# Routed attention and a gated long convolution: keys stored negated, one mask instruction, and a new hand-out of work in the last batch

## The chip, the cores and the metric

One core of one Trainium2 chip runs the whole program. Its five engines run side by side, each from a queue of its own: TensorE (PE, the matmuls), VectorE (DVE), ScalarE (ACT), GpSimd (POOL) and SyncE (SP, which here only starts transfers). The metric is the device time of one execution in microseconds (us); a profile of one execution gives in addition the span from the first to the last instruction and a record of each of them.

## The reference

Four batches, eight heads, 768 positions of 64 numbers. Queries and keys are each assigned to the nearest of 16 centroids of their head; a query sees the keys of its own cluster alone. The attention's output, heads side by side as 512 columns, goes through a projection to three parts, of which the middle one is convolved over the whole sequence with a long filter (a circular convolution by Fourier transform), and the three are multiplied and projected out.

```python
q_assign = np.argmax(np.einsum('bhsd,hcd->bhsc', q_n, c_n), axis=-1)
k_assign = np.argmax(np.einsum('bhsd,hcd->bhsc', k_n, c_n), axis=-1)
mask = q_assign[:, :, :, None] == k_assign[:, :, None, :]
scores = scale * np.matmul(q, k.transpose(0, 1, 3, 2))
scores = np.where(mask, scores, -1000000000.0)
scores = scores - np.max(scores, axis=-1, keepdims=True)
attn = np.exp(scores)
attn = attn / (np.sum(attn, axis=-1, keepdims=True) + 1e-09)
return np.matmul(attn, v).astype(np.float32)
...
proj = x @ w_proj
x1, x2, x3 = (proj[..., :D], proj[..., D:2 * D], proj[..., 2 * D:])
X2 = np.fft.rfft(x2, n=S, axis=1)
H = np.fft.rfft(filter_fft, n=S, axis=0)[None, :, :]
x2_conv = np.fft.irfft(X2 * H, n=S, axis=1)
y = x1 * x2_conv * x3
return (y @ w_out).astype(np.float32)
```

## The kernel before

**A planner writes the order.** The program is a list of 1943 operations, each with its engine or a choice of engines, a cost in us, a due time, and what it reads and writes. `place` (line 123) simulates the engines and gives each operation its engine and its place: an engine takes, among what could start first, what is due earliest. The result is the order of every engine's queue. Two dictionaries steer it: `NUDGE` (line 42) shifts the due time of each operation, by its number in the list, and `ONLY` (line 43) fixes the engine of 134 operations that could run on several. An operation with `lock=True` takes part in a rule between DVE and POOL: a POOL operation with a lock is made to wait for the last DVE operation with a lock that stands before it in the order, so that the two don't use the memory of the core together.

**Routing** (`routing`, line 574; `first_masks` for the first group). The heads are taken in eight groups of four heads, each as two pairs. Queries and keys are loaded, transposed on PE (L594, L607), copied out of PSUM as f32 (`copy`, L282 on ACT, L284 on DVE) and cast to bf16 into the score operands `T.augs` (again `copy`; ACT, DVE or POOL). There are 64 such casts, half of them for queries (`j` = 0), half for keys (`j` = 1). The similarity to the centroids is a matmul (L627); the largest of 16 gives a one-hot row for each position. A matmul with a triangular matrix (L647) breaks ties: in its result the winner is -1 and the rest 0 or more. From this the mask rows `T.ohT` are written, in two chunks of 384 columns: rows 64 to 127 (keys) as one at the winner and zero else, rows 0 to 63 (queries) as -BIG plus BIG at the winner, with BIG = 262144. They differ, so two instructions write each chunk (L653 on ACT or L655 on DVE), 28 in the seven groups behind the first. Small transfers put the 16 rows of each head under the 64 rows of its cast operand (L497).

**Scores and values** (`attention`, line 663). The mask costs no pass of its own: the score matmul contracts over 64 + 16 rows, so a score of another cluster is 262144 lower and its exponential is zero. For each of the 96 blocks of 128 keys, PE makes three banks of scores (L84), ACT takes their exponential with scale 1/8 (L694, L697), PE multiplies with the values in f32 (L708), and DVE adds the exponentials up for the denominators (L725 for the first two blocks of a pair of heads, on DVE or POOL; L729 for the others).

**The second stage** (`hyena`, line 817), once for each batch: U projects the middle part (L843) into sums and differences (L857, L862); `spectrum4` transforms it with matmuls into six banks, three row blocks `i` by real and imaginary part `cs`. Each bank is multiplied by two rows of the filter's spectrum straight out of PSUM (L873, DVE alone, 12 a batch), and L877 combines the products into `T.y`. For each of four column blocks `dt` and two halves `ch`, G makes the two gates: the third part is copied to SBUF (L914), the first is multiplied into it straight out of PSUM (L917, DVE alone). The inverse transform `I` and its folds (L942 to L954) give the convolution, L959 multiplies it by the gates (in the last batch by halves, on DVE alone), and W projects out (L990), followed by a copy and the store. The first three batches do this beside the attention of the next ones; behind the last attention only the last batch is left, with a rest of the batch before.

The program uses PSUM as eight banks; a bank is free for the next matmul when its last reader is through, so a late reader on DVE or ACT holds PE.

Of the kernel before, what the change touches and what calls it, by code (L numbers as in the profile page):

```python
# [27 lines left out]
BIG = 262144.0  # L28
# [236 lines left out]
def build(T):  # L265
# [7 lines left out]

    def ring(n, pr):
        return (2 * n + pr) % 3

    def A(i):
        return T0 + TAU1 * min(i, NE) + TAU2 * max(i - NE, 0)

    def copy(e, out, in_):  # L280
        if e == "ACT":
            T.nc.scalar.copy(out, in_)  # L282
        else:
            (T.nc.vector if e == "DVE" else T.nc.gpsimd).tensor_copy(out, in_)  # L284

    columns = lambda *a: product(T, *a)

    def ap(h):
        return bank(h.ids[0])

    def bank(i):
        return T.bank[i][:]

    def T_(name, i):
        return lambda: getattr(T, name)[i]

    def two(h):
# [8 lines left out]
    def alu(e):  # L306
        return T.nc.vector if e == "DVE" else T.nc.gpsimd
# [194 lines left out]
    def first_masks(pr):  # L502
# [35 lines left out]
        if pr == 0:  # L538
            for j in (1, 0):
                h2 = Bank("head")  # L540

                def rows(e, j=j, h2=h2):
                    o = ap(h2).bitcast(BF16)
                    for t in range(NT):
                        for hp in range(2):
                            T.nc.tensor.transpose(o[64 - 64 * hp:80 - 64 * hp, ts(t, 128)], oh()[:, 4 * t + 2 * j + hp], T.identb)
                op(("PE", .35), rows, due + 1.0 + .1 * (1 - j), r=[("oh", 0), "identb"], w=[h2], alloc=h2, kind="sim")
                for hp in range(2):
                    def put(e, j=j, hp=hp, h2=h2):
                        rs = slice(64 - 64 * hp, 80 - 64 * hp)  # L550
                        o, x = T.augs[0][hp][j][rs], ap(h2).bitcast(BF16)[rs, :S]
                        if j:
                            copy(e, o, x)
                        elif e == "ACT":
                            T.nc.scalar.activation(o, x, Act.Copy, scale=BIG, bias=-BIG)
                        else:
                            V().tensor_scalar(o, x, BIG, -BIG, op0=Alu.mult, op1=Alu.add)
                    got = op({"ACT": .8, "DVE": .55}, put, due + 1.2 + .3 * hp, r=[h2, ("zero", 0, j)],
                             w=[("augm", 0, hp, j)], free=[h2])
            return [got]  # L560
# [13 lines left out]
    def routing(n):  # L574
# [5 lines left out]
        for u in range(8):  # L580
# [30 lines left out]
            if ch == 1:  # L611
                for hp in range(2):
                    op({"ACT": .82, "DVE": .65, "POOL": .95}, lambda e, a=ring(n, pr), hp=hp, j=j, z=z: copy(
                        e, T.augs[a][hp][j][64 * hp:64 * hp + 64],
                        T.qkT[z][64 * hp:64 * hp + 64].rearrange("p a b -> p (a b)")), due + 8 if n else due + 6,
                       r=qk(z, 0) + qk(z, 1) + [("zero", ring(n, pr), j)],
                       w=[("aug", ring(n, pr), hp, j)], lock=True)
# [27 lines left out]
        for ch in range(2):  # L645
            h = Bank(cls)
            op(("PE", .165), lambda e, ch=ch, h=h: columns(ap(h)[:, :384], T.tri[:], T.ohB[:, ts(ch, 384)], True, True), due - 2 + .1 * ch,  # L647
               r=["ohB", "tri"], w=[h], alloc=h, kind="proj")
            for j in (1, 0):
                def hits(e, ch=ch, j=j, h=h):  # L650
                    o, x = T.ohT[64 * j:64 * j + 64, ts(ch, 384)], ap(h)[64 * j:64 * j + 64, :384]
                    if e == "ACT":
# [631 lines left out]
```

## Time and profile before

| | |
|---|---|
| median of 3 runs | 370.66 us (370.66 to 370.85) |
| the profiled execution | 370.64 us |
| its span, first to last instruction | 368.9 us |
| granted TensorE clock | 1.000 throughout |
| read from and written to HBM | 31.59 and 7.40 MB |
| costliest on PE | L708, values: 143.0 us of 768 matmuls |
| on ACT | L697 and L694, exponentials: 108.7 and 57.4 us |
| on DVE | L729, sums: 112.8 us of 64 additions |
| on POOL | L284, casts: 25.9 us of 29 |

Busy times of an engine count the time in which at least one of its instructions runs. In a wait, the line after the arrow is the one whose end released the line before it; then come the total, the number and the longest. In a time line, a figure in brackets is the idle time of the engine just before the instruction, with what released it.

### The profile page before, as it was taken

To read this page: it belongs to the slowest core of one execution; us is meant where nothing else is said; L and a number is where in the kernel's file an instruction comes from. 1 tells how busy PE (TensorE), PEld (TensorE's weight loads), DVE (VectorE), ACT (ScalarE), POOL (GpSimd) and SP (SyncE) were. 2 spreads that over 40 slices of the span, in tenths; PEclk is the share of its full clock that TensorE was granted. 3 is DMA by queue.
4 is the path that set the end of the run, shared out by engine and by line. 5 is a ranking of instruction groups with operands and counts; after the bars stand their busy time and mean duration, and the time that the engine had idled before them with its cause. 6 is when DMAs were issued, how large, how long until landed. Compare 5 with 4: busy or idle time off the path is not lost.

```text
span 368.9 us, 8653 instructions
## 1 busy us (share of the span) xinstructions
PE 357.5 (97%) x3314; PEld 208.9 (57%) x3316; DVE 342.5 (93%) x478; ACT 263.6 (71%) x495; POOL 120.9 (33%) x162
## 2 busy tenths in 40 slices
PE   7899999999999999999999999999999999999985
PEld 4455544555856565565555555566555655566672
DVE  7999999896999899999999999998998999999994
ACT  7998978877986859769869765899584785433242
POOL 7730730422032752331530044352221334016610
PEclk9999999999999999999999999999999999999999
DMA  7986597484247768748556964667477750110124
GB/s 175 202 189 126 128 211 195 93 189 110 62 80 156 115 156 169 152 103 129 107 64 183 238 170 81 146 152 98 81 116 167 150 77 1 48 45 2 59 115 171
DMA packets 90405, 46.20 MB, mean 125 GB/s; under 512 B 78248, under 2 KB 84092, under 8 KB 90364
## 3 DMA queue, kind: packets, MB, share of 16 engines
q1 hardware_dynamic: 85500, 36.15, 40.5%
q0 software_dynamic: 2752, 8.98, 17.1%
q10 hardware_dynamic: 2112, 0.52, 0.6%
q8 instruction: 26, 0.43, 0.5%
q14 instruction: 15, 0.12, 0.1%
HBM read 31.59 MB, written 7.40 MB: 106 GB/s over the span
## 4 chain that ended last, share of the span: by engine, by line
PE 78%; DVE 11%; ACT 5%; issue 3%; DMA 1%; POOL 1%; SPq 0%; DVEq 0%; ACTq 0%; POOLq 0%
PE bank L84 33%; PE pair L708 28%; PE bank L843 5%; PE bank L594 5%; DVE acc L729 3%; PE bank L627 2%; ACT p L697 1%; PE bank L82 1%; DMA qkraw<-in_k_dram 1%; DVE qkP L284 1%; PE bank L475 1%; PE bank L742 1%; ACT p L694 1%; PE bank L607 1%; DVE ohT L655 1%
## 5 line engine op out<-in xcount | busy, mean ns | idle before, releaser
L708 PE MATMUL pair<-p,vraw 128*64 128x385 f32 x768 | 143.0, 489 | 0.1
L697 ACT ACTIVATE p<-bank 128x512 f32<-128x512 f32 x192 | 108.7, 606 | 23.5 <-PE bank L84 16.0
L729 DVE TENSOR_TENSOR acc<-p,acc 128x1536 f32<-128x1536 f32 x64 | 112.8, 1762 | 3.2 <-ACT p L694 0.5
L84 PE MATMUL bank<-aug,aug 80*64 80x512 bf16 (+3 forms) x736 | 81.9, 327 | 2.1 <-ACT p L697 0.9
L708 PEld LDWEIGHTS pair<-p,vraw 128*64 128x64 f32 x768 | 56.6, 136 | 43.8 <-issue 36.7
L84 PEld LDWEIGHTS <-aug 80*64 80x64 bf16 (+1 forms) x736 | 45.6, 109 | 41.0 <-issue 26.3
L694 ACT ACTIVATE p<-bank 128x512 f32<-128x512 f32 x96 | 57.4, 606 | 5.4 <-PE bank L84 3.6
L284 POOL CAST aug<-qkP 64x768 bf16<-64x768 f32 x29 | 25.9, 900 | 83.3 <-DVE acc L729 55.9
L762 POOL DMA_DIRECT2D acc<-acc x30 | 24.4, 824 | 69.8 <-DMA acc<-acc 37.4
L84 PE MATMUL bank<-xT,wpj 128*64 128x384 bf16 x504 | 47.2, 326 | 0.0
L84 PEld LDWEIGHTS <-wpj 128*64 128x64 bf16 x504 | 30.2, 110 | 14.1 <-issue 2.6
L282 ACT COPY qkP<-bank 128x512 f32<-128x512 f32 (+1 forms) x46 | 23.1, 559 | 15.9 <-PE bank L594 9.7
L84 PEld LDWEIGHTS <-y 128*64 128x64 bf16 x472 | 24.0, 110 | 13.2 <-issue 3.6
L725 POOL TENSOR_TENSOR acc<-p,p 128x512 f32<-128x512 f32 x15 | 19.3, 1297 | 32.3 <-DVE acc L729 10.4
L873 DVE TENSOR_TENSOR tm<-bank,hm 128x512 f32<-128x512 f32 x44 | 28.1, 681 | 1.9 <-POOL uv L862 0.8
L84 PE MATMUL bank<-wout,y 128*64 128x512 bf16 (+1 forms) x200 | 24.0, 371 | 1.1 <-DVE y L959 1.1
L282 ACT CAST aug<-qkP 64x768 bf16<-64x768 f32 x28 | 23.2, 830 | 1.0 <-DVE qkP L284 0.4
L843 PE MATMUL bank<-wpj,xT 128*64 128x512 bf16 x192 | 22.7, 379 | 0.4 <-ACT p L697 0.4
L725 DVE TENSOR_TENSOR acc<-p,p 128x512 f32<-128x512 f32 x33 | 21.6, 690 | 0.4 <-DMA dd<-acc 0.4
L877 POOL TENSOR_TENSOR y<-tm 128x512 bf16<-128x512 f32 x14 | 17.8, 1277 | 12.8 <-DVE tm L873 10.6
L732 ACT COPY osb<-pair 128x770 f32<-128x770 f32 x16 | 12.9, 806 | 10.8 <-PE pair L708 10.7
L594 PEld LDWEIGHTS bank<-ident,qkraw 128*128 128x128 f32 x144 | 15.6, 141 | 6.3 <-ACT p L694 2.4
(178 smaller groups left out, 435.7 us busy)
## 6 DMA issues: line engine op xcount, KB each, us to landing
vraw<-in_v_dram SPq DMA_DIRECT2D x16, 384.0 KB, 5.2
qkraw<-in_q_dram SPq DMA_DIRECT2D x30, 192.0 KB, 3.9
rb<-dr SPq DMA_DIRECT2D x30, 192.0 KB, 3.7
qkraw<-in_k_dram SPq DMA_DIRECT2D x28, 192.0 KB, 3.6
out_dram<-ob SPq DMA_DIRECT2D x9, 512.0 KB, 5.0
acc<-acc POOLq DMA_DIRECT2D x10, 384.0 KB, 4.8
acc<-acc POOLq DMA_DIRECT2D x10, 192.0 KB, 4.2
y<-in_moe_filter_fft_dram SPq DMA_DIRECT2D x4, 384.0 KB, 4.3
```

Of the source, the lines that this page charges most:

```text
L84: T.nc.tensor.matmul(out[64 * i:64 * i + 64], lhsT[:, 64 * i:64 * i + 64], rhs, start=start, stop=stop)
L282: T.nc.scalar.copy(out, in_)
L284: (T.nc.vector if e == "DVE" else T.nc.gpsimd).tensor_copy(out, in_)
L594: T.nc.tensor.transpose(bank(h.ids[i // 4])[:, ts(i % 4, 128)], raw(ss[i // NT], i % NT), T.ident[:, ::-1] if 3 <= i < NT else T.ident)
L694: T.nc.scalar.activation(o, ap(h).rearrange("p (a b) -> p a b", a=2), Act.Exp, scale=0.125)
L697: T.nc.scalar.activation(flat(s)[:, lo:lo + 512], ap(h), Act.Exp, scale=0.125)
L708: T.nc.tensor.matmul(o[64 * hp:64 * hp + 64, ch, :385], T.vraw[vs][:, hp, sk * D:(sk + 1) * D], T.p[slots[sk]][:, hp, 384 * ch:384 * ch + ...
L725: alu(e).tensor_tensor(o, x, y, op=Alu.add)
L729: T.nc.vector.tensor_tensor(T.acc[os], T.p[slots[sk]][:, :, :S], T.acc[os], op=Alu.add)
L762: op(("POOL", .8), lambda e, rows=rows: T.nc.gpsimd.dma_start(flat_()[:rows], flat_()[rows:2 * rows], accum_op=Alu.add), te, r=[], w=AK, b ...
L843: T.nc.tensor.matmul(ap(h)[64 * i:64 * i + 64], T.xT[xs][:, kt, c:c + 64], T.wpj[:, kt, DM:2 * DM], start=kt == 0, stop=kt == ND - 1)
L873: op(("DVE", .68), lambda e, i=i, cs=cs, r=r, h=h: T.nc.vector.tensor_tensor(T.tm[r][:, cs], ap(h), hmrow(i, (0, 2, 2, 3)[2 * r + cs]), op ...
```

## The change

- Keys are cast with a factor -1 (`minus` in place of `copy`), and the exponential takes the scale -1/8 in place of 1/8. The signs of the mask follow: query rows are BIG at a miss and 0 at a hit. With this sign both halves of a chunk are a relu of scale times the matmul's result plus bias, with a scale and a bias for each row, so one instruction on ACT writes all 128 rows; 28 mask instructions become 14. The two columns `T.hs` and `T.hb` are written at the start by POOL.
- In the last batch, the imaginary banks of the first two row blocks are copied to SBUF first (by ACT or DVE), into `T.acc[0]`, and their four products may run on POOL or DVE. The first-part gates of the first two column blocks are copied likewise into `T.x3`, and their four products may run on either. So may the eight last products (L959).
- The costs that the planner assumes for the casts and for L725 on DVE are changed a little, and all of `NUDGE` and `ONLY` is new (1936 operations, 136 fixed engines). The operations that stay are the same, in another order and partly on other engines.

```diff
-NUDGE = {0:-244.575,1:-2716.133,...}
-ONLY = {13:"POOL",14:"POOL",15:"POOL",...}
+NUDGE = {0:-600.355,1:-451.825,...}
+ONLY = {15:"POOL",16:"POOL",18:"POOL",...}
...
+    def minus(e, out, in_):
+        if e == "ACT":
+            T.nc.scalar.activation(out, in_, Act.Copy, scale=-1.0)
+        else:
+            alu(e).tensor_scalar(out, in_, -1.0, None, op0=Alu.mult)
...
-                    op({"ACT": .82, "DVE": .65, "POOL": .95}, lambda e, a=ring(n, pr), hp=hp, j=j, z=z: copy(
+                    op({"ACT": .83, "DVE": .56, "POOL": .9}, lambda e, a=ring(n, pr), hp=hp, j=j, z=z: (minus if j else copy)(
...
-            for j in (1, 0):
-                def hits(e, ch=ch, j=j, h=h):
-                    o, x = T.ohT[64 * j:64 * j + 64, ts(ch, 384)], ap(h)[64 * j:64 * j + 64, :384]
-                    if e == "ACT":
-                        T.nc.scalar.activation(o, x, Act.Relu if j else Act.Copy, scale=-1.0 if j else -BIG, bias=0.0 if j else -BIG)
-                    else:
-                        V().tensor_scalar(o, x, -1.0 if j else -BIG, 0.0 if j else -BIG, op0=Alu.mult, op1=Alu.max if j else Alu.add)
-                op({"ACT": .47, "DVE": .55}, hits, due - 1.6 + .1 * ch, r=[h], w=[("ohT", j, ch)], free=[h])
+            op({"ACT": .57}, lambda e, ch=ch, h=h: T.nc.scalar.activation(
+                T.ohT[:, ts(ch, 384)], ap(h)[:, :384], Act.Relu, scale=T.hs, bias=T.hb), due - 1.6 + .1 * ch,
+               r=[h, "hit"], w=[("ohT", 0, ch), ("ohT", 1, ch)], free=[h])
...
-                        T.nc.scalar.activation(flat(s)[:, lo:lo + 512], ap(h), Act.Exp, scale=0.125)
+                        T.nc.scalar.activation(flat(s)[:, lo:lo + 512], ap(h), Act.Exp, scale=-0.125)
...
-                    op({"DVE": .63, "POOL": 1.5}, part, due - 1 + .2 * u, r=[("p", slots[i], u) for i in range(2)], w=[("acc", os, u)], lock=True)
+                    op({"DVE": .68, "POOL": 1.5}, part, due - 1 + .2 * u, r=[("p", slots[i], u) for i in range(2)], w=[("acc", os, u)], lock=True)
...
+                away = last and cs and i < 2
+                if away:
+                    spec, sk = (lambda i=i: T.acc[0][:].rearrange("p a b -> p (a b)")[:, ts(i, 512)]), [("acc", 0, i)]
+                    op(EV512, lambda e, spec=spec, h=h: copy(e, spec(), ap(h)), due + 1, r=[h], w=sk, free=[h])
+                else:
+                    spec, sk = (lambda h=h: ap(h)), [h]
                 for r in range(2):
...
+                    op({"DVE": .68, "POOL": 1.4} if away else ("DVE", .68), lambda e, i=i, cs=cs, r=r, spec=spec: alu(e).tensor_tensor(
+                        T.tm[r][:, cs], spec(), hmrow(i, (0, 2, 2, 3)[2 * r + cs]), op=Alu.mult), due + 1 + .1 * r,
+                       r=sk + [("hm", i, ((0, 2), (2, 3 if i == 0 else 0))[r][cs])], w=[("tm", r, cs), ("tm", r)],
+                       free=[] if away else [h], lock=away)
...
+                    elif last and dt < 2:
+                        op(EV384, lambda e, ch=ch, dt=dt, h=h: copy(e, T.x3[dt][:, ch], ap(h)[:, :384]), due + .8,
+                           r=[h], w=[("x3", dt, ch)], free=[h])
+                        op({"DVE": .55, "POOL": 1.1}, lambda e, ch=ch, dt=dt, x3=x3: alu(e).tensor_tensor(
+                            x3()[:, ch], T.x3[dt][:, ch], x3()[:, ch], op=Alu.mult), due + 1.4,
+                           r=[("x3", dt, ch)], w=xkeys[ch], lock=True)
...
-                op(("DVE", .55) if last else {"DVE": .95, "POOL": 2.1}, lambda e, dt=dt, ch=ch, cols=cols, x3=x3, yy=yy: alu(e).tensor_tensor(
+                op({"DVE": .55, "POOL": 1.1} if last else {"DVE": .95, "POOL": 2.1}, lambda e, dt=dt, ch=ch, cols=cols, x3=x3, yy=yy: alu(e).tensor_tensor(
...
+        def hit(e):
+            for j in range(2):
+                G().memset(T.hs[64 * j:64 * j + 64], -1.0 if j else BIG)
+                G().memset(T.hb[64 * j:64 * j + 64], 0.0 if j else BIG)
+        op(("POOL", .4), hit, 16, w=["hit"])
```

## The prediction

> **What bounds the kernel now.** I read the page first, its busy rows and its chain of waits.
>
> ```profile
> PE 357.5 (97%) x3314; PEld 208.9 (57%) x3316; DVE 342.5 (93%) x478; ACT 263.6 (71%) x495; POOL 120.9 (33%) x162
> ...
> PE 78%; DVE 11%; ACT 5%; issue 3%; DMA 1%; POOL 1%; SPq 0%; DVEq 0%; ACTq 0%; POOLq 0%
> ```
>
> TensorE (PE) works 357.5 of 368.9 us and holds 78% of the chain. The change touches no matmul: the scores, the value products, the gates and the transforms keep their number and their shapes. So whatever it takes off VectorE (DVE) or ScalarE (ACT) shortens the kernel only where PE now stands still. Where that is I read from the busy time of each engine in stretches of 12 us; the columns are PE, PEld, DVE, ACT, POOL, clock, DMA share, GB/s.
>
> ```profile
> 0.00:12.00 12.00, 9.20 (x46) 4.72 (x47) 9.30 (x28) 8.70 (x17) 8.99 (x41) 1.00 0.82 185
> 12.00:24.00 12.00, 11.25 (x114) 6.63 (x113) 11.29 (x22) 11.38 (x23) 7.33 (x20) 1.00 0.88 188
> 24.00:36.00 12.00, 11.25 (x98) 6.69 (x96) 11.21 (x12) 10.85 (x23) 0.82 (x1) 1.00 0.74 156
> ...
> 60.00:72.00 12.00, 11.57 (x93) 6.27 (x92) 10.92 (x15) 10.49 (x20) 3.42 (x3) 1.00 0.56 130
> ...
> 108.00:120.00 12.00, 11.53 (x97) 6.91 (x94) 11.79 (x13) 8.33 (x17) 3.23 (x4) 1.00 0.81 160
> ...
> 240.00:252.00 12.00, 11.25 (x132) 8.21 (x128) 11.34 (x16) 10.94 (x21) 5.02 (x5) 1.00 0.72 158
> ...
> 348.00:360.00 12.00, 10.93 (x178) 8.33 (x176) 11.85 (x24) 5.04 (x11) 3.40 (x3) 1.00 0.22 90
> 360.00:369.00 9.00, 4.63 (x44) 2.08 (x40) 3.46 (x8) 2.52 (x5) 0.00 (x0) 1.00 0.47 175
> ```
>
> PE's holes, twelve (or nine) minus the first busy number: 2.80 and 0.75 at the start, 0.75 in 24 to 36, 0.43 in 60 to 72, 0.47 in 108 to 120, 0.75 in 240 to 252, 1.07 in 348 to 360, 4.37 at the end. The stretches left out add 0.15. That is 11.54 us, the whole budget. The 4.37 is mostly the last eviction and the last store behind the last matmul, which the change leaves; most of the 2.80 is the wait for the first loads. In play are about 4.2 us between 12 and 360, and some of the 2.80.
>
> Two of the holes have a name in the waits of PE:
>
> ```profile
> PE bank L84 <- DVE y L959: 1.1, 1, 1.1
> ...
> PE bank L84 <- DVE ohT L655: 0.7, 1, 0.7
> ```
>
> **The merged mask instruction.** Each of the seven later routings writes its masks with four instructions, two for each half of the rows: L653 and L655, 28 in all.
>
> ```profile
> L655 DVE TENSOR_SCALAR ohT<-bank x7: 542/560/561, 32.6 to 280.7; 64x384 bf16<-64x384 f32 x7
> ...
> L653 ACT ACTIVATE ohT<-bank x21: 471/485/500, 31.4 to 269.5; 64x384 bf16<-64x384 f32 x21
> ```
>
> They take 21 x 0.485 + 7 x 0.560 = 14.1 us. Afterwards 14 instructions on ACT alone write all 128 rows of 384 elements, with scale and bias from columns. No row shows that form. Below it lies the plain 128x384 ACT copy of L282 (0.48); above it the 128x512 activation with a scale column of L451 (0.688). I take 0.58, near the middle: 14 x 0.58 = 8.1 us (6.7 to 9.6). Six us of engine time go, 3.9 of them DVE's. Almost all of it is hidden, since PE is full beside it. It shows once: at 32.58 two L655 run on DVE, held until two accumulations of L729 (29.04, 3.62 us) are through; ACT's second mask waits 0.8 for the bank and PE's next score stands 0.66. With masks on ACT alone nothing of this queue is left, so I count -0.7 (0 to -0.75, the whole hole of 24 to 36). What ACT does instead, 0.58 in place of 0.485, delays the exponentials queued behind it by 0.1, which PE has banks to ride out. The four column writes of the new constants run on GpSimd (POOL), like L1044's 0.09 each: some 0.3 us, needed only at 31 us, where POOL has stood 3.7 us idle before 20.3. Nothing; uncovered, it is +0.3.
>
> **Negated keys.** 32 of the 64 casts into the score operands become a multiplication by -1. On ACT the form is in the trace: L1069 writes 64x768 bf16 from f32 as an activation in 0.83, the cast of L282 takes 0.831. On DVE the cast takes 0.548; the nearest multiplication from SBUF, L381 with 128x384, takes 0.41, which doubled is 0.82: 0.55 to 0.82, and I take the cast, the row of the same shape. On POOL the cast takes 0.82, a two-input 128x512 operation 1.277, or 1.9 for 768: 0.82 to 1.9, and I take 0.82, since there is still one input. The sign in the exponential costs no instruction; L697's 0.602 stays. So 0, with +0.8 on the dear side, should one slow POOL cast in the start lie before the first scores (the rows at 14.67 and 15.76).
>
> **The last batch.** Two spectral results and four gate results are first copied to SBUF, by ACT at 0.587 and 0.480: 2 x 0.59 + 4 x 0.48 = 3.1 us. ACT is busy 8.03 of the 23 us from 337 to 360, so they are hidden; on DVE they would be 3.6. Then up to four spectral products (0.68), four gate products (0.55) and all eight last products (0.55) may go to POOL. The dictionary of fixed engines names one spectral product and one gate product for POOL; of the others the diff doesn't tell. Those two take 0.62 + 0.47 = 1.1 us off DVE, by the distance between starts in a train (4 products of L873 in 2.47; 2 of L917 in 1.01). DVE is busy 22.71 of 23.00 there, so this arrives at its end, and its end holds PE:
>
> ```profile
> 357.87 0.28 PE L84 MATMUL bank<-wout,y 128*64 128x256 bf16 x2
> 359.22 5.41 PE L84 MATMUL bank<-wout,y 128*64 128x256 bf16 x54 [1.07 <-DVE y L959]
> ```
>
> PE waits 1.07 for a product of L959, then works through the output projection without a pause. More than 1.07 can't be won here: without the wait PE itself is the end. I take -0.7, two thirds, because POOL's price comes back in part (next). Bounds: -1.07 and +2.4 (rival 2).
>
> A row speaks against these moves. A DVE operation with two inputs in SBUF is stretched when POOL works beside it: L729 goes from 1.754 to 2.592, L725 from 0.684 to 1.022. One with an input in PSUM isn't: L873 stays at 0.68, though most of its 48 run beside POOL. The copies turn PSUM inputs into SBUF ones, and the kernel makes such POOL operations wait for the DVE ones (the lock). The Trainium skill says the same in general (GPSIMD Engine Reference, section 4.1, Engine selection): elementwise work belongs on VectorE, about twice as slow on GpSimd for two inputs; this trace has 1.277 against 0.685, a ratio of 1.9. By that rule the tail would gain nothing and the sum would be -0.7 instead of -1.4.
>
> **The new order.** All due times change and some 170 engine choices are set, freed or set otherwise. PE's work stays at 357.5 minus or plus a few changes of array shape (a value product behind a transpose takes 1.45, else 1.30). What an order can still win are the holes without a name: 0.43 + 0.47 + 0.75 in the middle and perhaps 1 us at the start; what it can lose is as much. I take 0, -1.6 to +1.6.
>
> **Sum.** Profiled execution 370.64, its span 368.9, 1.7 around it; the median is 370.66, so the two agree. -0.7 (masks) + 0 (keys) - 0.7 (tail) + 0 (order) = -1.4: 369.2; I write 369.3.
>
> **Rivals.**
> 1. *The order pays the gain back.* The two named holes go, and others of their size open elsewhere, since PE has only 0.15 us of idle in the 22 stretches left out above and any late operand shows at once. For it: the waits of PE are ten rows of different places, nine of them a single wait each. Against: nothing in the diff adds work to PE's operands. One new hole like that of 240 to 252 (0.75), and another of 0.47: 369.3 + 1.2 = 370.5.
> 2. *GpSimd comes late in the last batch: slower.* A moved spectral product is a copy (0.59) and then 1.277, instead of 0.68 from PSUM: 1.2 us later, and the combination of L877 behind it (1.276 on POOL) waits for both. If two of the four go this way, one behind the other, the inverse transform of the first columns, at 352 now, moves by 2.4. PE's other work there (gates, the batch before) is finite, and POOL is free only while no two-input DVE operation holds the lock. It decides from about 1.1 us, where the delay exceeds what DVE's relief gives. For it: L877 on POOL already waits 10.6 us in sum for L873. Against: POOL lies idle from 350.4 to 356.9. Price 2.4 without the tail's gain, masks kept: 370.64 - 0.7 + 2.4 = 372.3.
> 3. *The order closes unnamed holes too.* Half of the 1.65 in the middle and 0.5 at the start: 369.3 - 1.3 = 368.0. For it: 6 us fewer of mask work on DVE and ACT, and both are above 10.8 of 12 in 24 to 36 and 240 to 252. Against: in 108 to 120 ACT has room (8.33 of 12), and PE still has its hole.
> 4. *The relief lands nowhere*: the masks leave ACT's place to other work and POOL gets what never held PE, 370.6.
>
> **Chances.** Forecast 0.40, rival 1 0.14, rival 2 0.20, rival 3 0.18, rival 4 0.08. What a measurement can tell from no change is 0.2%, 0.74 us, so the borders are 369.9 and 371.4. The forecast gives 0.38 faster and 0.02 same, rival 3 all faster, rivals 1 and 4 0.02 faster, 0.17 same and 0.03 slower, rival 2 slower but for 0.01: faster 0.58, same 0.20, slower 0.22. The forecast's own range is 368.6 to 369.9; to leave out no more than 2 in 10 I go down to 367.8, the better half of rival 3, and up to 371.7, into rival 2.
>
> **What would show it.** Masks: 14 instructions of 128x384 on ACT at 0.55 to 0.6, no mask on DVE, and PE's hole in 24 to 36 under 0.2. Keys: rows on ACT at 0.83 and on POOL at 0.82; 1.5 or more there would be the dear bound. Tail: DVE's 22.7 of 23.0 down by 1 us, and the 1.07 before the last output projections below 0.4; if instead PE stands around 350 to 353, before the first inverse transform, rival 2 holds. Order: the sum of PE's holes between 36 and 348 (2.0 with the small ones) shows by how much; above 3 it is rival 1, below 1 rival 3. A PE busy time off 357.5 by over 1 us would make the whole argument wrong, as the work of PE would not be constant.

## The result, and the profile after

| | before | after |
|---|---|---|
| median | 370.75 us (370.66 to 371.15) | 383.28 us (379.08 to 384.84) |
| ratio | | 1.0298, 95% interval 1.0208 to 1.0388: slower |
| profiled execution, span | 370.64, 368.9 | 382.15, 380.4 |
| PE busy, PE idle in the span | 357.5, 11.4 | 361.7, 18.7 |

369.3 was forecast, 367.8 to 371.7 the range, 22 in 100 the chance of slower. The ratio leaves out the execution of 384.84, which counts as slow. The executions of the changed kernel lie far apart, and the clock granted to PE differs among them (a mean of 0.991 to 0.999 over the span; 0.997 to 1.000 in the kernel before). The clock explains a part of it at most: two executions at 0.996 take 382.15 and 384.42, which is 3.1 and 5.3 us more than the one at 0.999, while a mean that is lower by 0.003 over 380 us makes about 1.1 us of PE's work.

The page of the changed kernel, its busy rows and its chain of waits:

```profile
PE 361.7 (95%) x3325; PEld 213.2 (56%) x3326; DVE 341.2 (90%) x473; ACT 265.0 (70%) x492; POOL 132.1 (35%) x166
...
PE 58%; DVE 17%; DMA 8%; issue 6%; ACT 3%; SPq 3%; POOL 2%; ACTq 0%; POOLq 0%; DVEq 0%
```

PE has fallen from 78% of the chain to 58, and 8% of it are now transfers. The busy time in stretches of 12 us, columns as before (PE, PEld, DVE, ACT, POOL, clock, DMA share, GB/s):

```profile
12.00:24.00 12.00, 10.29 (x74) 5.97 (x72) 9.85 (x18) 9.36 (x22) 9.41 (x26) 0.86 0.74 172
24.00:36.00 12.00, 10.95 (x116) 6.31 (x112) 9.80 (x14) 11.86 (x23) 5.78 (x5) 1.00 0.73 152
36.00:48.00 12.00, 12.00 (x104) 6.37 (x102) 11.69 (x11) 11.54 (x23) 2.75 (x5) 1.00 1.11 207
48.00:60.00 12.00, 10.24 (x86) 5.72 (x83) 10.64 (x12) 8.44 (x16) 3.61 (x3) 1.00 0.73 178
...
84.00:96.00 12.00, 10.93 (x88) 5.46 (x84) 10.49 (x11) 7.43 (x14) 2.39 (x3) 1.00 0.39 98
...
252.00:264.00 12.00, 10.39 (x128) 7.33 (x125) 10.47 (x17) 9.10 (x19) 5.01 (x4) 1.00 0.55 79
```

These rows show the holes of PE: 1.71, 1.05, 1.76, 1.07 and 1.61 us, where in the same stretches of time it had 0.75, 0.75, 0, 0.04 and 0 before. POOL is busy 9.41 us of 12 in 12 to 24 (7.33 before), the clock there is 0.86, and in 36 to 48 the transfers are at 1.11 (0.59 before), just ahead of the hole of 48 to 60. The new operations among the groups of instructions (busy us, mean ns, then idle time before them):

```profile
L290 POOL TENSOR_SCALAR aug<-qkP 64x768 bf16<-64x768 f32 x11 | 23.4, 2131 | 42.4 <-DVE acc L726 17.3 <-PE bank L84 16.3 <-DVE acc L730 3.5
...
L284 POOL CAST aug<-qkP 64x768 bf16<-64x768 f32 x16 | 14.0, 876 | 31.6 <-DVE acc L730 13.0 <-DVE dn L776 12.6 <-DVE dn L774 4.5
L288 ACT ACTIVATE aug<-qkP 64x768 bf16<-64x768 f32 x11 | 9.3, 841 | 1.2 <-DVE qkP L284 1.0
L655 ACT ACTIVATE ohT<-bank,hb,hs 128x384 bf16<-128x384 f32 x14 | 9.0, 674 | 5.3 <-PE bank L84 4.1 <-DMA rb<-dr 1.1
```

A key on POOL costs 2.13 us as a multiplication, a copy of the same shape 0.88 on the mean; the merged mask takes 0.674. The waits of PE, and the time line of its last work:

```profile
PE bank L84 <- DVE y L973: 2.0, 3, 1.0
PE bank L84 <- DMA vraw<-in_v_dram: 1.8, 1, 1.8
PE bank L84 <- ACT x L282: 1.3, 2, 1.0
```

```profile
369.50 0.87 PE L84 MATMUL bank<-wout,y 128*64 128x512 bf16 x4 [1.02 <-DVE y L973]
371.03 3.20 PE L84 MATMUL bank<-wout,y 128*64 128x512 bf16 x30 [0.66 <-DVE y L973]
374.56 1.82 PE L84 MATMUL bank<-wout,y 128*64 128x512 bf16 x20 [0.33 <-DVE y L973]
```

Where one wait of 1.07 stood before the last output projections there are three, 2.01 in sum. The 1.8 us is put down to a load of values; in the first experiment the same matmuls wait for the mask rows, and that wait goes when the loads around the mask rows are moved.

### The profile page after: what moved, and what is told of

Its sections match the earlier page's. It is cut to its first block, busy times and chain, and to the rows that moved or that the text cites. A ratio compares the mean times of both kernels' runs of the same rounds, so it can differ in the third digit from the quotient of the medians.

```text
span 380.4 us, 8658 instructions
## 1 busy us (share of the span) xinstructions
PE 361.7 (95%) x3325; PEld 213.2 (56%) x3326; DVE 341.2 (90%) x473; ACT 265.0 (70%) x492; POOL 132.1 (35%) x166
## 3 DMA queue, kind: packets, MB, share of 16 engines
q10 hardware_dynamic: 2944, 1.15, 1.2%
## 4 chain that ended last, share of the span: by engine, by line
PE 58%; DVE 17%; DMA 8%; issue 6%; ACT 3%; SPq 3%; POOL 2%; ACTq 0%; POOLq 0%; DVEq 0%
PE bank L84 26%; PE pair L709 18%; DVE acc L730 4%; PE bank L844 4%; PE bank L600 3%; DMA y<-in_moe_filter_fft_dram 3%; SPq L503 2%; DMA vraw<-in_v_dram 2%; PE bank L633 2%; DVE acc L726 2%; DVE y L973 1%; DMA qkraw<-in_q_dram 1%; POOL acc L726 1%; DVE qkP L284 1%; DMA dn<-dd 1%
## 5 line engine op out<-in xcount | busy, mean ns | idle before, releaser
L84 PE MATMUL bank<-aug,aug 128*64 128x256 bf16 (+3 forms) x732 | 81.3, 327 | 5.7 <-DMA vraw<-in_v_dram 1.8
L709 PEld LDWEIGHTS pair<-p,vraw 128*64 128x64 f32 x768 | 57.7, 136 | 41.7 <-issue 34.7
L84 PEld LDWEIGHTS <-aug 128*64 128x64 bf16 (+1 forms) x732 | 47.8, 109 | 41.1 <-issue 25.1
L84 PE MATMUL bank<-xT,wpj 128*64 128x384 bf16 x512 | 48.2, 326 | 0.2
L84 PEld LDWEIGHTS <-wpj 128*64 128x64 bf16 x512 | 31.5, 110 | 15.8 <-issue 5.5
L290 POOL TENSOR_SCALAR aug<-qkP 64x768 bf16<-64x768 f32 x11 | 23.4, 2131 | 42.4 <-DVE acc L726 17.3
L880 DVE TENSOR_TENSOR tm<-bank,hm 128x512 f32<-128x512 f32 x41 | 26.2, 683 | 0.9 <-POOL y L885 0.3
L284 POOL CAST aug<-qkP 64x768 bf16<-64x768 f32 x16 | 14.0, 876 | 31.6 <-DVE acc L730 13.0
L282 ACT COPY x<-bank 128x384 f32<-128x384 f32 x24 | 11.2, 478 | 12.2 <-PE bank L84 8.1
L885 POOL TENSOR_TENSOR y<-tm 128x512 bf16<-128x512 f32 x12 | 15.2, 1279 | 12.8 <-DVE acc L730 4.6
```

Source lines behind the costliest of these rows:

```text
L84: T.nc.tensor.matmul(out[64 * i:64 * i + 64], lhsT[:, 64 * i:64 * i + 64], rhs, start=start, stop=stop)
L290: alu(e).tensor_scalar(out, in_, -1.0, None, op0=Alu.mult)
L709: T.nc.tensor.matmul(o[64 * hp:64 * hp + 64, ch, :385], T.vraw[vs][:, hp, sk * D:(sk + 1) * D], T.p[slots[sk]][:, hp, 384 * ch:384 * ch + ...
L880: op({"DVE": .68, "POOL": 1.4} if away else ("DVE", .68), lambda e, i=i, cs=cs, r=r, spec=spec: alu(e).tensor_tensor(T.tm[r][:, cs], spec( ...
```

## The experiments

My theory after the result was that three things add up: GpSimd's multiplications, bulk loads that the new order lays onto small transfers, and the moves of the last batch. The rival was that the new order is bad as a whole and the parts don't matter. Below, "block" counts the 96 value products of PE; the lag of a block behind the kernel before tells where time goes.

**The multiplication taken out of the changed kernel.**

```diff
     def minus(e, out, in_):
+        elif e == "POOL":
+            T.nc.gpsimd.tensor_copy(out, in_)
```

> The changed kernel, with its order untouched, but the 11 key casts on GpSimd are plain casts again (those key halves are not negated). Theory A (the multiplication on GpSimd, 2.13 us in place of 0.82, makes the scores late, in the start above all): most of the 12 us go, 371 to 374 us, first value product near 25 us in place of 29.0, and the times of single runs lie close together again. Theory B (the new order itself and the moves in the last batch cost it): 378 us or more.

377.44 us (377.01 to 382.0), ratio 1.020 (1.0139 to 1.026): under theory B's range and above theory A's. The first block starts at 26.69 us instead of 29.03 (24.63 before). Those 2.3 us come from a buffer: ACT's copies of the transposed queries and keys write a tile that POOL's third multiplication (19.53, 2.13 us) still reads. ACT in the changed kernel, then in this run:

```profile
21.69 3.16 ACT L282 COPY qkP<-bank 128x384 f32<-128x384 f32 x8 [0.93 <-POOL aug L290]
```

```profile
19.31 3.21 ACT L282 COPY qkP<-bank 128x384 f32<-128x384 f32 x8
```

In this profile the large wait has its true name: PE waits for mask rows under a score operand, while POOL has started the four loads of w_proj in the middle of their transfers. Time lines of PE, POOL's queue and SP's queue in this run:

```profile
49.05 1.06 PE L84 MATMUL bank<-aug,aug 80*64 80x512 bf16 x10 [2.75 <-DMA aug<-ohT]
```

```profile
35.55 2.16 POOL L1107 DMA_DIRECT2D wpj<-in_moe_w_proj_dram  x4 [0.32 <-POOL wpj L1104]
```

```profile
33.51 3.11 SPq L505 DMA_DIRECT2D aug<-ohT  x5
...
38.11 3.39 SPq L505 DMA_DIRECT2D aug<-ohT  x3
```

Eight transfers of 24 KB each, of which the slowest measured lands 8.7 us after its issue (9.3 in the changed kernel, 1.9 in the one before), with the 3.1 MB of w_proj started between them. In the kernel before, the loads left at 43.43 to 46.4, behind the last mask row.

**The multiplication put into the kernel before.**

```diff
-lambda e, a=ring(n, pr), hp=hp, j=j, z=z: copy(
+lambda e, a=ring(n, pr), hp=hp, j=j, z=z: (times if j else copy)(
```

> The kernel before, its order untouched, but its 14 key casts on GpSimd are a multiplication by 1.0 (the same values). Theory A: 14 x 1.3 us more on GpSimd, in part in front of scores: slower by 4 to 10 us, 375 to 381. Theory B: GpSimd is idle two thirds of the time and hides it, within 1 us of 370.7.

374.33 us (373.89 to 375.35), ratio 1.0084 (1.0064 to 1.0104): +3.5 us against 370.85 beside it, a little under theory A's 4 to 10. The lag is 0.9 at the first block, 2.5 at the 21st, 4.0 at the 41st and 4.7 at the 85th. In none of these steps does PE wait for a late key. In the start VectorE's cast and multiplication beside POOL's work take 0.85 and 0.96 us (0.55 and 0.34 before), so its copy for the centroid products comes late and PE waits 0.89. At the 21st block SP is held by a load of queries, 7.69 us where it took 1.14 before, with the loads of w_proj just started on POOL:

```profile
46.52 7.69 SPq L329 DMA_DIRECT2D qkraw<-in_q_dram  x1
```

The small transfer of the reciprocals behind it is late, VectorE waits 1.83 for their broadcast, and PE 1.45; the next experiment has the same chain. At the 41st block two multiplications on POOL (4.65 us for what took 1.70) stand ahead of a combination of spectral products; VectorE waits 2.18 for it and PE 1.24. At the 85th PE waits 0.65 for VectorE, which waited for a broadcast.

**The merged mask alone, in the order before.**

```diff
-            for j in (1, 0):
-                def hits(e, ch=ch, j=j, h=h):
+                T.nc.scalar.activation(T.ohT[:, ts(ch, 384)], ap(h)[:, :384], Act.Relu, scale=T.hs, bias=T.hb)
```

> The kernel before, its order untouched, with the one mask instruction on ScalarE alone at the place of the first of the two; the signs of the masks and of the exponential's scale follow, the keys stay as they are (the negation is left out, so the scores have the wrong sign). Theory of the prediction: the wait behind two accumulations at 32.6 us goes, 0 to -0.7 us, 370.0 to 370.7. Rival: one instruction later on ScalarE, behind its exponentials, delays the masks: +0.3 us or more.

371.97 us (371.52 to 373.91), ratio 1.003 (1.0017 to 1.0044). The kernel leaves the negation out, so its scores have the wrong sign. It leads by 0.38 us at the 17th block: PE's wait for VectorE's masks is gone, as the prediction said, though 0.33 of the hole of 0.66 stays. At the 21st it lags by 1.44. SP's queue and PE in this run:

```profile
46.65 6.53 SPq L335 DMA_DIRECT2D qkraw<-in_q_dram  x1
53.28 2.85 SPq L340 DMA_DIRECT2D vraw<-in_v_dram  x1
56.17 0.47 SPq L786 DMA_DIRECT2D dr<-dn  x1
```

```profile
68.85 0.85 PE L752 MATMUL bank<-acc,ones 128*32 128x384 f32 x8 [1.74 <-DVE acc L739]
```

In the kernel before, the same load of queries (45.23) took SP 1.14 us and the small transfer of the reciprocals left at 53.76. Now SP is held 6.53 us, the reciprocals leave at 56.17, DVE's product that needs their broadcast waits 2.1 us, and the accumulation queued behind it holds PE 1.74.

**The moves of the last batch alone, in the order before.**

```diff
+                    if away and i == r == 1:
+                        P.moved.append(o)
...
+    for o in plan.moved:
+        o.on, o.lock = "POOL", True
```

> The kernel before, its order untouched, with the moves of the last batch alone: two spectral banks and four gate banks copied to SBUF by ScalarE first, one spectral product and three gate products on GpSimd as in the changed kernel, the other such products on VectorE from the copy. Theory of the prediction: VectorE's train ends 1 to 2 us earlier, PE's wait before the last output projections falls from 1.07 to under 0.4: 369.9 to 370.3. Rival 2: GpSimd or the lock comes late and PE waits longer there or before the first inverse transform: 371.5 to 373.

373.7 us (373.6 to 373.76), ratio 1.0071 (1.0056 to 1.0086). The one last product that the changed kernel gives to POOL stays on DVE here. Up to the last block the lag is 0.1 to 0.3; the rest comes behind it. DVE stands 2.12 us, up to 350.58, for POOL's combination of the spectral products, and PE has two new waits beside the old one:

```profile
352.39 0.84 PE L84 MATMUL bank<-xT,wpj 128*64 128x384 bf16 x8 [1.02 <-DVE qkP L933]
354.31 1.26 PE L84 MATMUL bank<-inv,y 128*64 128x192 bf16 x26 [1.00 <-DVE y L888]
361.71 5.41 PE L84 MATMUL bank<-wout,y 128*64 128x256 bf16 x54 [1.05 <-DVE y L977]
```

**The weight loads later** (in the changed kernel with plain copies; the times are the planner's, the loads left at 55, twice at 74, and at 94).

```diff
+    when = iter((60.0, 70.0, 80.0, 88.0))
+    for o in order:
+        if o.fn.__name__ == "load_wpj":
+            o.start = next(when)
```

> This is the changed kernel with its 11 GpSimd key copies made plain, not negated (as in the first experiment, 377.44 us, so the routing is computed with keys of the wrong sign there), and with the four loads of w_proj (786 KB each) issued later, after the mask rows of the second group instead of among them. Theory A, that the new order lays the weight loads onto the mask-row transfers (landing 1.9, 5.6 and 8.7 us after their issue in the first experiment, 1.8 to 1.9 before) and PE stands for it: the transfers land in about 2 us again, the idle time of PE that ended with the transfer into aug (2.7 us at its longest, 3.6 in sum) goes, and the time is 374.0 to 375.5 us. Rival B, that another load or the order itself holds the transfers: landings stay over 5 us and the time stays within 1 us of 377.4. Rival C, that the weights are then late for the output projections: a new wait of PE on the weight tile, and 377 us or more.

380.63 us (379.52 to 381.35), against the expectation. But the lag at the 17th block is -0.4 where the first experiment had +2.3: the wait at 49 is gone, 2.7 us. Then 4 us are lost against the first experiment between the 21st and the 29th block, with a wait of 2.05 us at 85.07 for keys: the two loads at 74 met the loads of keys and queries. Theory A held for the place that I took the loads from, and failed for the one that I put them in.

**The tail put back, and all three repairs.**

```diff
-op(EV512, lambda e, spec=spec, h=h: copy(e, spec(), ap(h)), due + 1, r=[h], w=sk, free=[h])
+op(EV512, lambda e: None, due + 1, r=[h], w=sk, free=[h])
```

> The changed kernel with its 11 GpSimd key copies plain (keys of the wrong sign there), and the moves in the last batch undone: gates, spectral and last products are on DVE straight from PSUM, the copies into SBUF are dropped; the order is the changed one. Theory A, from the run of the kernel before with the tail moves alone (+2.85 us): the moves cost 1.5 to 3 us here too, and the time is 374.5 to 376 us. Rival B, that in the new order the tail has slack that hides them: 377.0 to 377.8 us. Rival C, that DVE is relieved in the tail of this order: 378 us or more.

> The changed kernel with three repairs together: 11 GpSimd key copies plain (keys of the wrong sign there), the four loads of w_proj issued later, and the moves of the last batch undone. What is left of the change is the merged mask, the negation on DVE and ACT, and the rest of the new order. Theory A, that the three causes add: 371.5 to 373.5 us. Rival B, that the new order has a loss of its own beyond the weight loads (the first value product was 2.06 us later than in the kernel before in the first experiment): 374 us or more, with the loss present already at the first value product.

380.34 (378.24 to 380.64) and 383.04 (382.35 to 383.58). These two tell nothing of the moves. By the edit the order gives the bank away where the copy stood, so without the copy a product multiplies what stands in the bank later, and the next matmul into the bank waits for it.

**ScalarE's masks and later loads, in the kernel before.**

```diff
+        if o.fn.__name__ == "hits" and o.start < 40:
+            o.on = "ACT"
+    when = iter((60.0, 70.0, 80.0, 88.0))
```

> The kernel before in its own order, with two edits: the two plain masks of the first routing that DVE wrote are written by ACT in their place, and the four loads of w_proj are issued later. Theory A: the hole of PE at 32 us that waits for DVE's masks closes (-0.4 us, as in the run of one merged mask up to the sixteenth value product), and the loads of the queries and of dr are no longer issued behind the bulk of the weights, so that nothing is given back: 369.9 to 370.5 us. Rival B, that the gain is given back at the next routing as in the run of one merged mask (371.97): 370.8 us or more, with a wait of DVE's broadcast of over 1.5 us at about 60 to 66 us. Rival C, that the weights come too late for the output projections: a new wait on them and 372 us or more.

373.85 us (372.34 to 375.77), ratio 1.0069 (1.0042 to 1.0097). No gain in time. The hole at 33 us is closed (the lag falls from 0.30 at the first block to -0.12 at the 17th and 21st), but there is a new wait of 1.52 us for queries at 82.41: again loads of weights on loads of queries.

**The changed kernel with two repairs.** Queries are negated where POOL has the keys, and the loads go into a gap of the transfers that the earlier run had shown (shares 0.10 and 0.02 at 60 to 68 us).

```diff
-(minus if j else copy)(
+(minus if j == turned(key) else copy)(
...
+    when = iter((60.0, 60.1, 60.2, 60.3))
```

> The changed kernel in full (nothing is left out), with two repairs: where GpSimd writes a pair's keys it copies them plainly and the pair's queries are negated instead, by ScalarE or VectorE; and the four loads of w_proj are issued behind GpSimd's accumulation at about 54 us, ahead of the 8 us in which the transfers of the earlier run with later loads stood nearly empty (shares 0.10 and 0.02 at 60 to 68). Theory A, that the loads on the mask rows cost 2.7 us and their second place in the earlier run cost 4 of its own by falling on the loads of keys: PE's wait of 2.7 us at 49 us and the one of 2.05 us at 85 us are both absent, and the time is 374.0 to 375.2 us. Rival B, that any later place costs as much as it gives: 376.5 us or more, with a new wait of PE on keys, queries or the weights. Rival C, that GpSimd's plain copies were not the cause of the 6 us of the first experiment, but the missing sign: 379 us or more.

376.88 us (376.13 to 378.11), ratio 1.016 (1.0138 to 1.0182). The waits at 49 and at 85 are both absent. The time missed the range of theory A (374.0 to 375.2), and the new wait behind the loads that rival B named isn't there either. The start lost 1.2 us or more: six casts with the sign went from POOL to ACT (busy 269.8 against 264.8), and PE waits 0.83 for the filter at 20.29 and 1.15 for an exponential at 27.15.

**The same, with POOL's products of the last batch on DVE.**

```diff
+        if o in plan.tail:
+            o.on = "DVE"
```

> The same kernel, and the gate, spectral and last products of the last batch that GpSimd had (three, one and one) are on VectorE; ACT's copies into SBUF stay, since the order frees the banks with them. Nothing is left out. Theory A, that in the new order GpSimd's part of the tail is the late one (PE stood 1.02, 0.66 and 0.33 us before the last output projections): these waits shrink below 1.2 in sum and the time is 0.5 to 1 us under that of the kernel beside it. Rival B, that VectorE is full there and the relief was real: 1 to 2.5 us over it, with longer waits for the same products.

380.88 us (378.92 to 382.37): 4.0 over the run beside it by the medians, 1.5 by the profiled spans (377.2 and 375.7), of which the second holds a stretch at half clock; against that run's two executions at full clock (spans 374.4 and 374.6) it is 2.7. PE's waits for the last products grow from 2.0 to 2.7 and one of 0.63 for the combination appears. In the new order the relief of DVE by POOL's products was real; what ACT's copies cost or give there is not shown.

**Single operations.**

```diff
+        G.tensor_copy(b16[h], x[h])
+        G.tensor_scalar(b16[h], x[h], -1.0, None, op0=Alu.mult)
...
+        C.activation(b16[:, :384], ps[:, :384], Act.Relu, scale=hs, bias=hb)
```

> No part of the computation is done: this kernel measures single instructions, three times each, one engine after the other. On GpSimd, 64 rows of 768 from f32 to bf16: a plain copy, a multiplication by -1, an addition of 1; the multiplication with 384 columns, with 128 rows, with f32 output, with bf16 input; a product of two tensors. Then copy, multiplication and product of that shape on VectorE; then on ScalarE the mask form 128x384 from PSUM with scale and bias from columns, with the scale alone from a column, with constants, and the 64-row forms. Theory A, that GpSimd's multiplication by a constant is dear in itself: about 2.1 us where the copy takes 0.82, and in proportion to the columns; Rival B, that it was dear by what ran beside it: under 1.2 us here. For ScalarE, theory A: 0.67 us with two columns and 0.48 to 0.52 with constants, so that the columns cost the difference; rival B: all forms of 128 rows within 0.05 us.

The groups of this kernel, on POOL the copy, the products by a constant and by a tensor, then ACT's mask form with two columns, one and none:

```profile
L50 POOL TENSOR_SCALAR b<-x 64x768 bf16<-64x768 f32 x3 | 6.4, 2122 | 0.2
...
L58 POOL TENSOR_TENSOR b<-x,y 64x768 bf16<-64x768 f32 x3 | 5.4, 1793 | 0.2
L52 POOL TENSOR_SCALAR b<-x 64x384 bf16<-64x384 f32 x3 | 3.5, 1164 | 0.2
...
L49 POOL CAST b<-x 64x768 bf16<-64x768 f32 x3 | 2.4, 816 | 3.5 <-DMA x<-in_q_dram 3.4
L64 ACT ACTIVATE b<-ps,hb,hs 128x384 bf16<-128x384 f32 x3 | 2.0, 672 | 0.1
L66 ACT ACTIVATE b<-ps,hs 128x384 bf16<-128x384 f32 x3 | 1.7, 582 | 0.1
...
L65 ACT ACTIVATE b<-ps 128x384 bf16<-128x384 f32 x3 | 1.5, 491 | 0.1
```

The price is the operation's own. On POOL one input and a constant cost more (2.12) than two inputs (1.79); 128 rows cost the same as 64 (2.125), half the columns about half. On ACT each column operand adds 0.09 us.

**The merged mask with later loads, in the order before.**

```diff
+    when = iter((54.5, 54.5 + .01, 54.5 + .02, 54.5 + .03))
```

> The kernel before in its own order, nothing left out, with the merged mask on ScalarE, the keys negated by ScalarE and VectorE (the queries instead, where GpSimd copies the keys), the last batch as it was, and the four loads of w_proj behind GpSimd's accumulation at about 54 us instead of at 43 to 46. Theory A, that the merged mask gives 0.4 us and that the loss in the run of one merged mask (371.97) came from loads of queries stuck behind the weights in the queue: the issue of the queries at 46 us takes under 1.5 us, the wait of PE at 66 us is absent, and the time is 369.8 to 370.5 us. Rival B, that the weights now stand before other loads: 371.2 us or more, with a new wait of PE on keys, queries or values between 56 and 90 us.

372.12 us (371.64 to 372.48), ratio 1.0029 (1.0019 to 1.004). The marks of theory A are there: the load of queries at 46.52 takes 0.65, the wait at 66 is gone, and the lag falls by 0.2 from the first to the 17th block and does not rise at the 21st. Its time is not: the lag at the first block is 1.48. Where POOL had both operands of a pair, I gave the one with the sign to ACT, and two of these (0.84 us each, at 20.95 and 22.18) stand ahead of the first exponential, which starts at 24.43 instead of 23.03 in the run of one merged mask. So keeping the multiplication off POOL in this way costs the start more than the merged mask gives.

**Fillers at the start of the changed kernel.**

```diff
+                for _ in range(4 * (pr == 1 and ch == 0)):
+                    awake(h)
...
+            for _ in range(3 * (pr == 0)):
+                awake(h)
```

> The changed kernel, nothing left out, with seven matmuls on a constant tile (each 0.22 us at full clock, results overwritten) in the first routing: three where PE stood 0.73 us before the transposes at 14.39 us, four where it stood 0.94 us before the centroid products at 15.92. Theory A, that these two standstills, 1.67 us within 2.3, bring the clock of 0.50 that the profile of the changed kernel shows from 15.9 to 19.2 us and that this makes its executions uneven (379.08 at a mean clock of 0.999, 382.15 to 384.84 at 0.991 to 0.996): the rows from 15 to 20 us show a clock of 1.00, most executions lie at 0.998 or more, and the median is 379 to 380.5 us. Rival B, that the half clock comes whatever PE does there: clock of 0.50 again in the first 30 us and a median of 382 us or more.

383.06 us (380.61 to 384.67). Stretches of 3 us of the changed kernel, and the same of this one:

```profile
15.00:18.00 3.00, 2.08 (x8) 0.56 (x8) 2.97 (x7) 2.65 (x5) 2.92 (x9) 0.64 1.17 244
18.00:21.00 3.00, 3.00 (x23) 2.15 (x20) 1.22 (x4) 2.01 (x4) 2.85 (x3) 0.79 0.50 175
```

```profile
15.00:18.00 3.00, 2.35 (x19) 1.16 (x17) 2.97 (x7) 2.94 (x6) 2.92 (x9) 1.00 0.70 155
18.00:21.00 3.00, 3.00 (x24) 1.99 (x21) 2.15 (x6) 1.55 (x4) 2.85 (x3) 1.00 0.81 266
```

In the profiled execution the half clock is gone, yet the first block starts at 28.96 instead of 29.03: there PE had time to spare, POOL at 2.9 of 3.0 had not, and ACT's copies again wait 2.04 us for its third multiplication. And the executions are as uneven as before. Theory A fell in the part that matters.

**Plain copies and the loads at 55 us.** The changes of the first experiment and the later loads of the two repairs.

> The changed kernel with GpSimd's 11 key copies plain (keys of the wrong sign there, as in the first experiment, 377.44 us) and the four loads of w_proj behind GpSimd's accumulation at about 54 us, the place of the run with two repairs (376.88), but without that run's negated queries, which held PE 1.2 us longer in the first 28 us. Theory A, that the loads' old place costs 2.7 us and the negated queries took 1.2 of it back: first value product at 26.3 to 26.7 us as in the first experiment, no wait of PE over 1 us between 30 and 360, and 374.2 to 375.2 us. Rival B, that the place of the loads is worth less than its wait, since other work then ends later: 376 us or more with no such wait.

375.5 us (374.64 to 375.96), ratio 1.0114 (1.0094 to 1.0133), 1.9 us under the first experiment and 0.3 above theory A's range, with both of its marks. No wait of PE over 1 us is left between 30 us and the last output projections, and the lag at the 13th block is 2.4 where it was 5.4.

```profile
55.12 2.17 POOL L1108 DMA_DIRECT2D wpj<-in_moe_w_proj_dram  x4
```

## Why the prediction was wrong

The account, by profiled spans in which the rows show no clock of 0.50 while PE works: 379.3 (the changed kernel with fillers), 376.1 (plain copies on POOL), 374.2 (and the loads at 55), 368.9 (before). By these, 3.2 us are GpSimd's multiplications, 1.9 the place of the loads, and 5.3 the rest. The first term is known to some 2 us only: the one execution of the changed kernel itself at a mean clock of 0.999 has a span of 377.4, the three such of the first experiment 375.3 to 376.1, which makes 1.3 to 2.1. The medians (383.28, 377.44, 375.5 and 370.9) give 5.8, 1.9 and 4.6. Executions at a lower clock weigh in them (with fillers 381.01 at a mean clock of 1.000, 384.67 at 0.991, but also 380.61 at 0.995), and so does scatter that the clock doesn't explain.

- **Keys, "0", with 0.82 on POOL: the step that failed first.** I took the copy's row since "there is still one input", with 1.9 as the dear bound. Measured are 2.13, 2.12 by itself, beyond both ends, and +3.5 us in the order before. The page named in the prediction, the Trainium skill's GPSIMD Engine Reference, section 4.1 (Engine selection), calls one-input work on GpSimd roughly line-rate. The copy comes nearer to VectorE's time for the same work (0.82 against 0.55), the constant multiplication does not: 2.12, four times 0.55. The "+0.8, should one slow POOL cast in the start lie before the first scores" counted one cast; 4 of the 11 lie in the first 27 us. It also looked for the loss in a late key alone. The runs show it where other work waits for POOL: ACT for the buffer that the multiplication reads (2.3 us in the changed kernel), VectorE for the combination behind two of them, and SP for a load that a small shift put beside the weights.
- **Masks, -0.7.** The mechanism was right, PE's wait for the two masks on DVE goes: -0.38 us in the order before, where 0.33 of that hole stays. So the size came to about half. The instruction takes 0.674 instead of the 0.58 assumed (two column operands at 0.09 each). In that order the gain turned into a loss because the weights left 0.4 us earlier and the load of queries 1.4 us later, behind them. In the changed kernel the hole in 24 to 36 is 1.05, not under 0.2, but its waits there are for exponentials and for ACT's copies, not for masks.
- **The last batch, -0.7; rival 2 at +2.4.** In the order before rival 2 was right, +2.85 us, with the waits where the prediction put them (352 to 354) and DVE waiting for POOL. The prediction counted two products on POOL; the order gave it one spectral product, three gate products and one last product. In the new order the part is covered: taking POOL's products away again costs 1.5 to 4 us. The tail as a whole still idles more than before, by 0.8 us (6.15 against 5.35 of PE's idle behind 324 us, in the last experiment and before).
- **The order, 0, with -1.6 to +1.6.** This was the other failed step. I sized it by the holes that stood there to be won. The loss came in part from a thing that was not counted: four loads that the order moved from behind to among the mask rows. The prediction priced the order by PE's holes and followed no transfer. The mark of rival 1, "the sum of PE's holes between 36 and 348" above 3, was 7.4 us (1.8 before by the stretches, where the prediction wrote 2.0), but the multiplications and the loads are in it. With both out it was 3.7, which is 1.9 more than before, against rival 1's price of 1.2.
- **PE's time.** The sentence that a PE busy time off by over 1 us would break the argument applies: 361.7, and 359.8 with plain copies and later loads. The matmuls are nearly the same; twelve that used the whole array are split in two. In the order before, with POOL's casts as multiplications, the busy time rises by 1.7 (359.2), and 0.8 of it are the filler matmuls of the start: eleven of them took 0.6 us each instead of seven, before the rest took 0.38. So the busy time of the same work is not constant to 1 us, which the prediction took for granted.

What stays open: of the 5.3 us, 2.95 are idle time of PE in small pieces (0.3 up to 36 us, 0.5 to 108, 0.7 to 216, 0.7 to 324, 0.8 behind) and 2.3 are the longer busy time of nearly the same matmuls; no run separates the order's choices behind them, and none has the new order without the other changes. Nor is it settled how much of the scatter of the changed kernel the half clock makes. No version here beats the kernel before.

## What to carry to other kernels

Don't price an operation by its number of inputs or by a row of another opcode: on this chip a copy on GpSimd took 0.82 us and the same copy times -1 took 2.12, so a free sign on VectorE or ScalarE is not free on GpSimd. Ask also what waits behind an engine that is mostly idle: a buffer that it still reads held ACT and the first block by 2.3 us. When an order is made anew, follow the bulk loads first: 3.1 MB started 6 us earlier turned transfers of 1.9 us into transfers of up to 9, and PE stood 1.8 us, 2.7 with plain copies. And in an order tuned to the tenth, a gain of 0.4 us may move one load behind another and cost over four times as much.

## What the runs showed of the hardware

- A queue can be held by the transfers of another: SP took 6.53 us to issue one load of queries behind GpSimd's four loads and 7.69 in the run with POOL's multiplications, 0.65 with those loads moved away.
- VectorE's multiplication of 128x384 in SBUF at 11.68 us took 2.20 us in the changed kernel, where POOL's memsets of 0.73 us each run beside it; it took 0.74 with plain copies, where they are done by then, and 0.34 in the kernel before. No run tests them as the cause.
- PE's clock went to 0.50 for 3.4 us at a time, after standstills that were short: in the changed kernel 0.73 and 0.94 us with 0.58 of work between; in the run with two repairs one of 1.15 (at 27.15) and smaller ones; in the two runs with the tail put back 1.61 and 0.65. Much the same standstills brought none in the run with the products on DVE (1.14 at 26.76, 1.73 and 0.65 at 367.83), nor did a single one of 2.75 us at 49 us.
- The clock's records show what they have in common. In each of the 15 profiles of a whole kernel every drop, those behind the last matmul too, begins a whole number of stretches of 3.41 us after the start of the full clock (in the changed kernel 5.60 us, and the drop at 15.84, three stretches later). In such a stretch ahead of a drop PE stood 1.51 us or more by the profile's busy times. Every stretch with 1.99 us or more was followed by a drop, none with 1.48 or less, and between them both occur: 1.51 and 1.59 with a drop, 1.52 to 1.74 without. The 2.75 us at 49 us fall into two stretches, 1.36 and 1.39. What decides between 1.5 and 2 us stays open.
- The Trainium skill (TensorE: Matmul & The Clock Gate, Part 1: The HAM clock gate) gives a half-rate state, reached after an idle window, and a free-running window of about 3.4 us: the rate and the length agree, but ahead of four drops in the middle of the work PE was idle for only 1.51 to 2.06 us of such a stretch.
- None of the six profiles in the order before shows the half clock while PE works; four of the nine in the new order do. Executions without a profile point to it in the order before too: the run with ScalarE's masks and later loads has means of 0.993 to 0.995 in four of eight.
- The half clock need not cost much at the end. The run with two repairs had it and the one with the products on DVE had not; the first lagged behind the second by 0.4 us at the first block, 1.9 at the fifth and 0.6 at the last. Among the executions of the run with two repairs it does show: 376.13 and 376.36 us at 1.000, 377.41 and 378.11 at 0.995.
